# First rows transposed within the attention, first layer between the last routing steps, third set's gathers moved up

## The chip, the cores and the metric

The kernel runs on one core of one Trainium2 chip. The metric is the device time in microseconds (us) of one execution; lower is better. A time is the median of several executions. The engines are PE (TensorE), DVE (VectorE), ACT (ScalarE), POOL (GpSimd) and SP (SyncE, which only issues DMAs here).

## What is computed

A recurrent linear attention over 4 batches, 8 heads, 768 steps and head size 48, and on its output (3072 rows of 384) a mixture of 8 experts with one expert for each row:

```python
for t in range(S):
    cur = np.einsum('bhd,bhe->bhde', u[None] * kt, vt)
    y[:, :, t] = np.einsum('bhd,bhde->bhe', rt, state + cur)
    state = w[None, :, :, None] * state + np.einsum('bhd,bhe->bhde', kt, vt)
...
logits = x @ w_gate
expert_idx = np.argmax(logits, axis=1)
gate_w = probs[np.arange(N), expert_idx]
...
h = np.maximum(np.einsum('ecd,edf->ecf', disp, w1), 0.0)
y = np.einsum('ecf,efd->ecd', h, w2)
out[i] = gate_w[i] * y[expert_idx[i], pos[i]]
```

w1 is 8 x 384 x 1024 and w2 is 8 x 1024 x 384, all in float32.

## The kernel before

**Attention.** The 3072 rows are 24 tiles of 128 steps. The loop `for i in range(NI)` (L617) runs the attention of tile i and, one turn later, the gate of tile i-1. In each turn PE makes the scores of tile i+1 (`scores`, L521), a small product `c` (`mix`, L80 and L82) and, after ACT has copied `c` to `ct` (L87), a second small product, here called the **pull** (L92). DVE copies its result (L93): 8 gate logits of tile i-1, and the factors with which ACT writes the diagonal blocks of tile i+2's score matrix, eight instructions of `diag` (L502). PE then transposes the attention's output of tile i-1 back to rows (`turn`, tile `xp`, L104), and does `values1` (L555) and `values2` (L564) of tile i; ACT copies the outputs (`xs`, L568) and the rows (`xr`, `keep_rows`, L111). DVE masks the next scores (`masks`, L525), scales keys (`prep_keys`, L507; `prep_values`, L513) and keeps the state (`state_of`, L543).

**Routing.** Tiles go through the routing in groups; tiles 22 and 23 are groups by themselves. `route` (L124) is a generator of three parts: DVE finds the maximum and its one-hot `oh` (L127 to L140); PE ranks the rows (`rk`, L145 to L148) from `oh` and the running counts `lane`, which are then advanced (L151); DVE makes the row's slot and the softmax's divisor (L159 to L165). `advance()` runs one part. `scatters` writes the rows to `xsd` in device memory at their slots, by indirect DMA from POOL. `counts` (L178) and `places` (L185) turn the last counts into the row numbers `pidx` which `gather(k)` reads back, by POOL's indirect DMAs, into `xg[k % 2]`.

**Experts.** `PASSES` lists nine sets of rows: set 0 is the first 160 rows of expert 0, gathered already in turn 20 from what tiles 0 to 15 have sent (2 tiles of 128 rows, 80 of each used), set 1 the other 256 of expert 0, sets 2 to 8 are 416 rows each of experts 1 to 7 (4 tiles of 104). For each set `xtrans` transposes the gathered rows in three parts (tile `tp`, L290) and splits each into a high and a low half, `xh` on ACT (L294) and `xl` on DVE (L295); `layer1` makes 8 blocks `a` of 9 matmuls each (L307 to L309, three products for each of 3 parts of the contraction), which ACT and DVE split into `hh` (L312) and `hl` (L313); `layer2` makes three blocks `b` of 24 matmuls (L326 to L328); `finish` transposes them back (`yp`, L342) and scatters the rows to the output (L334). The first layer of set k, block by block, comes before the transposes of set k+1 and the second layer of set k.

**Weights.** `wstream` is a generator: by a plan, one step fetches a slice `wr` from SP (L240, four buffers) and splits earlier ones into high and low halves `ws`, the high on ACT (`CAST`, L248), the low on DVE (L249). For expert 0 one step runs at the end of a turn of the attention; its low half is issued in the next step. The experts after that run one step after each block.

**What sets the order.** The kernel is recorded under a manual schedule: each engine runs its instructions in the order in which the Python code issues them, and waits by semaphores. POOL's indirect DMAs stand in one queue with its arithmetic. PSUM tiles with one tag share buffers: `tp` and the blocks `a` of set 0 take turns in two buffers `a0`, with `u` and `y` as the third.

The end of the attention before: after the last turn come the transposes of set 0 (`acts`), the small product of tile 23 and the first block of layer one, then the pull of tile 23, the ranks of tiles 22 and 23, and the other blocks with `counts`, `places` and `gather(1)` after the second. `gather(k + 1)` stands at the head of the loop over the sets, so `gather(2)` comes after both transposes of set 0's output.

Of the kernel before, what the change touches and what calls it, by code (L numbers as in the profile page):

```python
# [7 lines left out]
F32R = mybir.dt.float32r  # L8
# [5 lines left out]
PSUM = bass.MemoryType.PSUM  # L14
# [20 lines left out]
def rwkv_moe(nc, tc, dmj, rkv, bdc, wv, wu, uv, wg, w1, w2, out, cap):  # L35
# [4 lines left out]
    with ExitStack() as ctx:  # L40
# [175 lines left out]
        with ExitStack() as mc:  # L216
# [7 lines left out]
            psB = pa.enter_context(tc.tile_pool(name="psB", bufs=1, space=PSUM))  # L224
            mc.enter_context(tc.manual_schedule())
            xg = [keep.tile([128, 4, XW], F32, name=f"xg{j}") for j in range(2)]
            wtiles = {}

            def wset(e):
# [387 lines left out]
            for i in range(NI):  # L617
# [37 lines left out]
                    T[i + 2]["bon"] = to  # L655
                xp = turn(i - 1, T[i - 1]["xs"], ps1)
                advance()
                each(prep_values, i + 2)
                state_of(i)
                values1(i)  # L660
                each(diag, i + 2, (0, 1, 2))
# [7 lines left out]
                    advance()  # L669
                if i == 1:  # L670
                    setup_ok(wc)
                next(ws)
                if i == 18:
                    early_places(sm, ps1)
                if i == 20:
# [2 lines left out]
                if i in (9, 13):  # L678
                    nc.gpsimd.memset(xg[i == 13], 0.0)
                T.pop(i - 1)  # L680
            lc.close()
            pa.close()
            psA = mc.enter_context(tc.tile_pool(name="psA", bufs=2, space=PSUM))
            buf = mc.enter_context(tc.tile_pool(name="act", bufs=1, side="right"))
            xh, xl = (buf.tile([128, 3, WL], F32R, name=n) for n in ("xh", "xl"))
            hh, hl = (buf.tile([128, 8, WL], F32R, name=n) for n in ("hh", "hl"))
            yt = buf.tile([128, 3, WL], F32, name="yt")
            scatters(NI)
            acts = [xtrans(0, j) for j in range(3)]
            take(0)  # L690
            c = mix(None, T[NI - 1]["xs"], ps1)
            acts[0]()
            ct = mixed(c, buf)
            acts[1]()
            acts[2]()
            first = layer1(0, 0)
            to = place_of(NI - 1, sm, rows_of)
            pull(c, ct, to)
            xp = turn(NI - 1, T[NI - 1]["xs"], ps1)
            advance()  # L700
            advance()
            rout(NI - 1, sm, ps1, rows_of, "rows")
            advance()
            keep_rows(NI - 1, xp, rows_of)
            first()
            advance()
            scatters(1)
            second = layer1(0, 1)
            advance()
            scatters(NI)  # L710
            counts(ps1)
            places(1, E, cs[:, 0:E], sm)
            gather(1)
            second()
            next(ws)
            next(ws)
            for f in (2, 3):
                layer1(0, f)()
                next(ws, None)
            ac.close()  # L720

            wsp.append(mc.enter_context(tc.tile_pool(name="wsq", bufs=1)))
# [9 lines left out]
            for d in range(3):  # L732
                layer2(0, d)
                next(ws)
            take(1)
            for d in range(3):
                xtrans(1, d)()
            finish(0, 0)
            finish(0, 1)
            for k in range(1, len(PASSES)):  # L740
                if k + 1 < len(PASSES):
                    gather(k + 1)
                for f in range(8):
                    layer1(k, f)()
                    next(ws, None)
                    if k > 1 and 1 <= f <= PASSES[k - 1][4]:
                        finish(k - 1, f - 1)
                if k + 1 == len(PASSES):
                    nc.gpsimd.drain()
                if k + 1 < len(PASSES):  # L750
                    take(k + 1)
                    for d in range(3):
                        xtrans(k + 1, d)()
                        layer2(k, d)
                        next(ws, None)
                        next(ws, None)
                    e = PASSES[k + 1][0] + 1
                    if e < E:
                        ws = wstream(e, PLAN)
                        next(ws)  # L760
                else:
                    layer2_last(k)
# [227 lines left out]
```

## Time and profile before

| what | us |
|---|---|
| median of 3 runs | 401.98 (399.9 to 402.25) |
| profiled execution, its own time | 398.83 |
| its span, from the first to the last instruction | 397.0 |

The profiled execution is one execution of the program; 1.83 us lie outside its span. All times inside it are counted from the span's start. The attention fills the span up to about 130 us, the experts the rest. "Granted clock" is the share of TensorE's 2.4 GHz that it was given: 1.00 is 2.4 GHz, 0.50 is 1.2 GHz. Busy time of a matmul overlaps that of its neighbours, so the step from one start to the next is the better measure of its cost. A wait is put down to the event that came last before the instruction.

### The profile page before, as it was taken

The numbers are of one execution on the slowest core, as the hardware profiler recorded it, in microseconds if no ns is written. First come the engines' busy times: TensorE is split into PE (matmuls) and PEld (weight loads), VectorE is DVE, ScalarE is ACT, GpSimd is POOL, SyncE is SP. The second block draws the span as 40 slices with busy tenths as digits, with TensorE's granted clock in tenths as the row PEclk, the third lists the DMA queues.
The fourth block names the chain that finished last, engine by engine and source line by source line (L and its number), as shares of the span: only waits on it lengthen the run. The fifth ranks groups of instructions, "written<-read, shape, count | busy, mean of one in ns | idle before, by whom it ended". The sixth has DMA issues, their size and how long they took to land.

```text
span 397.0 us, 9469 instructions
## 1 busy us (share of the span) xinstructions
PE 373.5 (94%) x3587; PEld 339.1 (85%) x3590; DVE 238.7 (60%) x574; ACT 203.9 (51%) x556; POOL 136.2 (34%) x199
## 2 busy tenths in 40 slices
PE   7999999999998799689999999999999999999993
PEld 3678777777886699689999999999999999999992
DVE  6897889898986775614745645645645645643210
ACT  3768787778776463414624724724724724722301
POOL 6122639565675321711501601601601601201203
PEclk9999999999999989969999999999999999999998
DMA  8999988888723463830633643644644644500102
GB/s 174 263 244 245 230 228 242 255 233 251 216 88 94 158 192 92 248 78 5 214 108 110 188 140 114 186 143 110 195 138 116 191 140 120 155 4 16 43 1 70
DMA packets 20632, 59.93 MB, mean 151 GB/s; under 512 B 4302, under 2 KB 4450, under 8 KB 20576
## 3 DMA queue, kind: packets, MB, share of 16 engines
q1 hardware_dynamic: 14848, 44.12, 40.6%
q0 software_dynamic: 5600, 14.72, 11.6%
q8 instruction: 30, 0.49, 0.6%
q10 hardware_dynamic: 128, 0.39, 0.4%
q14 instruction: 26, 0.21, 0.2%
HBM read 49.98 MB, written 10.03 MB: 151 GB/s over the span
## 4 chain that ended last, share of the span: by engine, by line
PE 61%; issue 13%; ACT 11%; DVE 7%; DMA 3%; POOL 2%; POOLq 1%; SPq 0%; DVEq 0%; ACTq 0%
PE a L307 8%; PE a L308 8%; PE a L309 8%; PE b L326 7%; PE b L327 7%; PE b L328 7%; ACT s L502 7%; PE a L521 3%; PE y L564 2%; DVE s L525 2%; PE tp L290 2%; PE yp L342 2%; POOL out L334 2%; PE c L92 2%; DMA xg<-xsd,pidx 2%
## 5 line engine op out<-in xcount | busy, mean ns | idle before, releaser
L334 POOL DMA_INDIRECT out<-yo,ids x32 | 32.2, 1008 | 176.2 <-ACT yo L333 174.9
L307 PE MATMUL a<-xh,ws 128*128 128x416 f32 (+1 forms) x216 | 75.7, 350 | 1.0 <-DVE xl L295 1.0
L326 PE MATMUL b<-hh,ws 128*128 128x416 f32 (+2 forms) x216 | 74.5, 345 | 0.0
L312 ACT ACTIVATE hh<-a 128x416 fp32r<-128x416 f32 (+1 forms) x72 | 35.2, 489 | 73.9 <-PE a L309 73.8
L308 PE MATMUL a<-xl,ws 128*128 128x416 f32 (+1 forms) x216 | 73.1, 338 | 0.0
L309 PE MATMUL a<-xh,ws 128*128 128x416 f32 (+1 forms) x216 | 73.1, 338 | 0.0
L328 PE MATMUL b<-hh,ws 128*128 128x416 f32 (+2 forms) x216 | 72.5, 336 | 0.0
L327 PE MATMUL b<-hl,ws 128*128 128x416 f32 (+2 forms) x216 | 72.5, 336 | 0.0
L313 DVE SCALAR_TENSOR_TENSOR hl<-a,hh 128x416 fp32r<-128x416 f32 (+1 forms) x72 | 39.9, 554 | 47.8 <-ACT hh L312 47.1
L249 DVE TENSOR_TENSOR ws<-wr,ws 128x384 fp32r<-128x384 f32 (+1 forms) x112 | 66.8, 612 | 0.2 <-ACT ws L248 0.2
L502 ACT ACTIVATE s<-eye,l 128x128 f32<-128x128 f32 x168 | 53.8, 391 | 20.1 <-DVE l L93 20.1
L248 ACT CAST ws<-wr 128x384 fp32r<-128x384 f32 (+1 forms) x112 | 59.9, 557 | 0.0
L329 DVE COPY yt<-b 128x416 f32<-128x416 f32 (+2 forms) x27 | 14.6, 542 | 70.3 <-PE b L328 70.3
L491 POOL TENSOR_TENSOR P<-dm 112x512 f32<-112x512 f32 x21 | 27.1, 1289 | 48.9 <-DVE dm L507 17.7
L294 ACT CAST xh<-tp 128x416 fp32r<-128x416 f32 (+1 forms) x27 | 12.7, 484 | 60.0 <-PE tp L290 60.0
L307 PEld LDWEIGHTS a<-xh,ws 128*128 128x128 f32 x216 | 41.3, 191 | 1.5 <-DVE xl L295 1.3
L326 PEld LDWEIGHTS b<-hh,ws 128*128 128x128 f32 x216 | 42.0, 194 | 0.2
L327 PEld LDWEIGHTS b<-hl,ws 128*128 128x128 f32 x216 | 41.9, 194 | 0.2
L328 PEld LDWEIGHTS b<-hh,ws 128*128 128x128 f32 x216 | 41.6, 193 | 0.4
L308 PEld LDWEIGHTS a<-xl,ws 128*128 128x128 f32 x216 | 41.4, 192 | 0.5 <-DVE xl L295 0.2
L309 PEld LDWEIGHTS a<-xh,ws 128*128 128x128 f32 x216 | 41.3, 191 | 0.4
L273 POOL DMA_INDIRECT xg<-xsd,pidx x32 | 34.9, 1091 | 13.9 <-issue 6.7
(147 smaller groups left out, 560.4 us busy)
## 6 DMA issues: line engine op xcount, KB each, us to landing
wr<-w SPq DMA_DIRECT2D x24, 512.0 KB, 4.4
wr<-w SPq DMA_DIRECT2D x32, 384.0 KB, 3.4
bd<-bdc SPq DMA_DIRECT2D x24, 384.0 KB, 5.0
dm<-dmj SPq DMA_DIRECT2D x40, 192.0 KB, 4.2
dm<-dmj SPq DMA_DIRECT2D x6, 256.0 KB, 7.7
xg<-xsd,pidx POOLq DMA_INDIRECT x32, 4.6
out<-yo,ids POOLq DMA_INDIRECT x32, 3.7
dm<-dmj ACTq DMA_DIRECT2D x2, 192.0 KB, 4.1
```

The source lines that it names most:

```text
L248: nc.scalar.copy(out=hi, in_=r)
L249: low.append(lambda: nc.vector.tensor_tensor(out=lo, in0=r, in1=hi.bitcast(F32), op=ALU.subtract))
L307: nc.tensor.matmul(a, lhsT=wh, rhs=xh[:, d, :n], start=d == 0, stop=False)
L308: nc.tensor.matmul(a, lhsT=wh, rhs=xl[:, d, :n], start=False, stop=False)
L309: nc.tensor.matmul(a, lhsT=wl, rhs=xh[:, d, :n], start=False, stop=d == 2)
L312: nc.scalar.activation(hh[:, f, :n], a, AF.Relu)
L313: nc.vector.scalar_tensor_tensor(out=hl[:, f, :n], in0=a, scalar=0.0, in1=hh[:, f, :n].bitcast(F32), op0=ALU.max, op1=ALU.subtract)
L326: nc.tensor.matmul(o, lhsT=wh, rhs=hh[:, f, :n], start=f == 0, stop=False)
L327: nc.tensor.matmul(o, lhsT=wh, rhs=hl[:, f, :n], start=False, stop=False)
L328: nc.tensor.matmul(o, lhsT=wl, rhs=hh[:, f, :n], start=False, stop=f == 7)
L334: r = nc.gpsimd.indirect_dma_start(out=out[:, :], out_offset=bass.IndirectOffsetOnAxis(ap=ids[k][0][:qo, i:i + 1], axis=0), in_=yo, in_off ...
L502: nc.scalar.mul(out=s[:, h, p], in_=eye, mul=bon)
```

## The change

Three things are moved; the arithmetic stays as it is.

1. In the attention the weight step `next(ws)` runs after the pull and the transposes of the rows, ahead of `diag`, where it stood at the end of the turn.
2. In the last turn the first two parts of set 0 are transposed and split ahead of `values1`, the third directly after the loop. `xh` and `xl` move to a pool that lives from the start, and the score buffers of PSUM are given to the experts in the middle of that turn. After it come block 0 of layer one, the small product of tile 23, block 1, the pull, the rank of tile 22, block 2, the rank of tile 23, and block 3 after `gather(1)`.
3. `gather(2)` is issued after the first block of set 0's second layer, ahead of set 0's output.

```diff
+            xh, xl = (keep.tile([128, 3, WL], F32R, name=n) for n in ("xh", "xl"))
...
                 advance()
+                next(ws)
                 each(prep_values, i + 2)
+                if i == NI - 1:
+                    pa.close()
+                    psA = mc.enter_context(tc.tile_pool(name="psA", bufs=2, space=PSUM))
+                    acts = [xtrans(0, j) for j in range(2)]
+                    take(0)
+                    acts[0]()
+                    acts[1]()
                 state_of(i)
...
-                next(ws)
...
+            xtrans(0, 2)()
             lc.close()
-            pa.close()
-            psA = mc.enter_context(tc.tile_pool(name="psA", bufs=2, space=PSUM))
             buf = mc.enter_context(tc.tile_pool(name="act", bufs=1, side="right"))
-            xh, xl = (buf.tile([128, 3, WL], F32R, name=n) for n in ("xh", "xl"))
...
+            first = layer1(0, 0)
+            c = mix(None, T[NI - 1]["xs"], ps1)
+            ct = mixed(c, buf)
             scatters(NI)
-            acts = [xtrans(0, j) for j in range(3)]
-            take(0)
-            c = mix(None, T[NI - 1]["xs"], ps1)
-            acts[0]()
-            ct = mixed(c, buf)
-            acts[1]()
-            acts[2]()
-            first = layer1(0, 0)
+            first()
+            second = layer1(0, 1)
             to = place_of(NI - 1, sm, rows_of)
             pull(c, ct, to)
             xp = turn(NI - 1, T[NI - 1]["xs"], ps1)
             advance()
-            advance()
             rout(NI - 1, sm, ps1, rows_of, "rows")
             advance()
             keep_rows(NI - 1, xp, rows_of)
-            first()
+            second()
+            third = layer1(0, 2)
             advance()
-            scatters(1)
-            second = layer1(0, 1)
+            next(ws)
+            advance()
+            third()
             advance()
             scatters(NI)
             counts(ps1)
             places(1, E, cs[:, 0:E], sm)
             gather(1)
-            second()
             next(ws)
-            next(ws)
-            for f in (2, 3):
-                layer1(0, f)()
-                next(ws, None)
+            layer1(0, 3)()
+            next(ws, None)
...
             for d in range(3):
                 layer2(0, d)
                 next(ws)
+                if d == 0:
+                    gather(2)
...
-                if k + 1 < len(PASSES):
+                if 1 < k < len(PASSES) - 1:
                     gather(k + 1)
```

In the orders below a number after a name is the buffer's; line numbers from L227 on are one or a few higher in the changed kernel.

ACT in turn 21 of the attention, before: the row copy, two casts of weights, the copy `ct`, then the next output copies.

```order
L111 COPY xr_121<-xp_2250 128x384
L248 CAST ws_0_1013<-wr_0_1370 128x384
L248 CAST ws_0_1013<-wr_0_1565 128x384
L87 COPY ct<-c 128x128
L568 COPY xs_2368<-y_0_2350 128x2x128
L568 COPY xs_2368<-y_1_2351 128x2x128
```

The same place now:

```order
L111 COPY xr_123<-xp_2252 128x384
L87 COPY ct<-c 128x128
L249 CAST ws_0_979<-wr_0_1522 128x384
L249 CAST ws_0_979<-wr_0_1700 128x384
L569 COPY xs_2374<-y_0_2356 128x2x128
L569 COPY xs_2374<-y_1_2357 128x2x128
```

The casts stand behind `ct` instead of ahead of it; in turns that still have a `diag`, they stand between `ct` and its first six instructions.

PE at the end of the attention, before, from the rank of tiles 20 and 21 on (blocks of layer one are shown by their first matmul):

```order
L148 MATMUL rk_2403<-lane,ones 128x16
...
L564 MATMUL y_1_2410<-s_120,bd_1924 48x128 x2
L290 MATMUL tp_0_2472<-idn,xg_101 128x128 x2
L290 MATMUL tp_1_2475<-idn,xg_101 128x128 x2
L290 MATMUL tp_2_2478<-idn,xg_101 128x128 x2
L82 MATMUL c<-xs_2427,wgz 32x128 x4
L307 MATMUL a_0_2498<-xh,ws_0_1011 128x256
...
L92 MATMUL c<-pick,ct 128x16
...
L145 MATMUL rk_2517<-oh_2446,tri 128x8
...
L145 MATMUL rk_2544<-oh_2535,tri 128x8
...
L307 MATMUL a_1_2551<-xh,ws_0_1011 128x256
```

PE there now:

```order
L148 MATMUL rk_2405<-lane,ones 128x16
L291 MATMUL tp_0_2418<-idn,xg_101 128x128 x2
L291 MATMUL tp_1_2421<-idn,xg_101 128x128 x2
...
L291 MATMUL tp_2_2473<-idn,xg_101 128x128 x2
L308 MATMUL a_0_2485<-xh,ws_0_977 128x256
...
L82 MATMUL c<-xs_2450,wgz 32x128 x4
L308 MATMUL a_1_2510<-xh,ws_0_977 128x256
...
L92 MATMUL c<-pick,ct 128x16
...
L145 MATMUL rk_2529<-oh_2469,tri 128x8
...
L308 MATMUL a_2_2545<-xh,ws_0_977 128x256
...
L145 MATMUL rk_2568<-oh_2561,tri 128x8
```

Block 1 (a_1) now stands ahead of the pull of tile 23, and block 2 (a_2) between the ranks of tile 22 and tile 23, which stood side by side.

DVE over the same stretch, before:

```order
L295 TENSOR_TENSOR xl<-tp_0_2472,xh 128x256
L295 TENSOR_TENSOR xl<-tp_1_2475,xh 128x256
L295 TENSOR_TENSOR xl<-tp_2_2478,xh 128x256
L93 COPY l_2508<-c 128x16
L159 TENSOR_TENSOR ps_2521<-rk_2517,oh_2446 128x8
...
L138 TENSOR_TENSOR oh_2535<-key_2531,km_2533 128x8
L140 TENSOR_TENSOR z_2537<-l_2508,mx_2529 128x8
L313 SCALAR_TENSOR_TENSOR hl<-a_0_2498,hh 128x256
L151 TENSOR_TENSOR lane<-lane,oh_2535 128x8
```

DVE now:

```order
L296 TENSOR_TENSOR xl<-tp_1_2421,xh 128x256
L159 TENSOR_TENSOR ps_2455<-rk_2405,oh_2385 128x16
...
L140 TENSOR_TENSOR z_2471<-l_2396,mx_2463 128x8
L296 TENSOR_TENSOR xl<-tp_2_2473,xh 128x256
L314 SCALAR_TENSOR_TENSOR hl<-a_0_2485,hh 128x256
L93 COPY l_2520<-c 128x16
...
L314 SCALAR_TENSOR_TENSOR hl<-a_1_2510,hh 128x256
...
L138 TENSOR_TENSOR oh_2561<-key_2557,km_2559 128x8
...
L250 TENSOR_TENSOR ws_0_980<-wr_0_1700,ws_0_979 128x384
L151 TENSOR_TENSOR lane<-lane,oh_2561 128x8
```

The third `xl` stands behind two parts of the routing, the low half of block 1 inside the chain of tile 23, and a weight subtraction ahead of the last `lane`.

POOL before, from the last scatters to the gathers of sets 2 (xg_101) and 3 (xg_102):

```order
L172 DMA xsd<-xr_123,slot 24576x400
L273 DMA xg_102<-xsd,pidx 128x400 x2
L334 DMA out<-yo_0_2818,ids_2481 3072x384
L334 DMA out<-yo_1_2827,ids_2481 3072x384
L273 DMA xg_101<-xsd,pidx 104x400 x4
L273 DMA xg_102<-xsd,pidx 104x400 x4
```

POOL there now:

```order
L172 DMA xsd<-xr_125,slot 24576x400
L274 DMA xg_102<-xsd,pidx 128x400 x2
L274 DMA xg_101<-xsd,pidx 104x400 x4
L335 DMA out<-yo_0_2830,ids_2424 3072x384
L335 DMA out<-yo_1_2839,ids_2424 3072x384
L274 DMA xg_102<-xsd,pidx 104x400 x4
```

Set 2's four gathers stand directly behind set 1's two, ahead of the two output scatters for which POOL has to wait.

## Rows read from the trace of the kernel before

**Rows 1.** Page, part 1: busy time, share of the span and instructions of each engine.

```profile
PE 373.5 (94%) x3587; PEld 339.1 (85%) x3590; DVE 238.7 (60%) x574; ACT 203.9 (51%) x556; POOL 136.2 (34%) x199
```

**Rows 2.** Waits of PE, 128 to 397 us: for whom, us in total, times, longest.

```profile
PE tp L290 <- DMA xg<-xsd,pidx: 4.7, 3, 2.4
PE rk L145 <- DVE oh L138: 1.9, 1, 1.9
PE a L307 <- DVE xl L295: 1.0, 1, 1.0
```

**Rows 3.** Timeline of PE, 160 to 180 us: start, us, instruction [idle before <- who ended it].

```profile
164.68 0.25 PE L290 MATMUL tp<-idn,xg 104*128 104x104 f32 x1
...
170.34 0.43 PE L290 MATMUL tp<-idn,xg 104*128 104x104 f32 x1 [0.94 <-DMA xg<-xsd,pidx]
170.47 0.56 PE L326 MATMUL b<-hh,ws 128*128 128x256 f32 x1
...
175.57 0.52 PE L290 MATMUL tp<-idn,xg 104*128 104x104 f32 x4
175.87 0.36 PE L326 MATMUL b<-hh,ws 128*128 128x256 f32 x1
...
178.81 0.52 PE L290 MATMUL tp<-idn,xg 104*128 104x104 f32 x4
```

**Rows 4.** Windows of 2 us; columns PE, PEld, DVE, ACT, POOL busy, PEclk, DMA share, GB/s.

```profile
138.00:140.00 2.00, 2.00 (x13) 2.00 (x13) 1.69 (x7) 1.19 (x3) 0.98 (x1) 0.50 0.31 111
146.00:148.00 2.00, 2.00 (x19) 2.00 (x18) 1.93 (x7) 1.83 (x5) 0.00 (x0) 1.00 0.60 166
168.00:170.00 2.00, 0.43 (x1) 0.18 (x1) 0.00 (x0) 0.00 (x0) 1.70 (x2) 0.63 1.02 283
```

**Rows 5.** Timeline of POOL, 95 to 200 us, around the indirect transfers.

```profile
142.32 1.05 POOL L273 DMA_INDIRECT xg<-xsd,pidx  x1 [2.52 <-DVE ws L249]
...
156.64 0.96 POOL L334 DMA_INDIRECT out<-yo,ids  x1 [11.95 <-ACT yo L333]
...
159.16 1.10 POOL L273 DMA_INDIRECT xg<-xsd,pidx  x1 [0.31 <-issue]
...
163.57 1.08 POOL L273 DMA_INDIRECT xg<-xsd,pidx  x1 [0.30 <-issue]
```

**Rows 6.** Instructions that write or read xg, 110 to 200 us: issue to landing.

```profile
DMA to landing us min/median/max: 2.9/4.6/7.6
```

**Rows 7.** Waits of PE, 25 to 128 us.

```profile
PE c L92 <- ACT ct L87: 3.2, 6, 1.0
```

**Rows 8.** Timeline of ACT, 48 to 72 us and 110 to 150 us.

```profile
55.74 1.86 ACT L502 ACTIVATE s<-eye,l 128x128 f32<-128x128 f32 x6 [0.70 <-DVE l L93]
...
126.92 0.94 ACT L248 CAST ws<-wr 128x384 fp32r<-128x384 f32 x2
127.75 0.29 ACT L87 COPY ct<-c 128x128 f32<-128x128 f32 x1
```

**Rows 9.** Timeline of PE, 112 to 148 us, at the boundary.

```profile
123.65 0.40 PE L92 MATMUL c<-pick,ct 128*128 128x16 f32 x2 [0.68 <-ACT ct L87]
...
128.09 0.40 PE L92 MATMUL c<-pick,ct 128*128 128x16 f32 x2 [0.95 <-ACT ct L87]
...
132.83 0.39 PE L307 MATMUL a<-xh,ws 128*128 128x256 f32 x1 [1.04 <-DVE xl L295]
...
136.73 0.17 PE L145 MATMUL rk<-oh,tri 128*128 128x8 bf16 x1 [1.92 <-DVE oh L138]
...
141.73 0.28 PE L307 MATMUL a<-xh,ws 128*128 128x256 f32 x1
```

**Rows 10.** Timeline of DVE, 128 to 138 us: parts of the routing chain.

```profile
129.07 0.17 DVE L159 TENSOR_TENSOR ps<-rk,oh 128x16 f32<-128x16 f32 x1 [0.37 <-PE rk L148]
...
130.04 0.14 DVE L127 TENSOR_REDUCE mx<-l 128x1 f32<-128x8 f32 x1
...
130.90 1.03 DVE L249 TENSOR_TENSOR ws<-wr,ws 128x384 fp32r<-128x384 f32 x2
```

## The prediction

> **What bounds the kernel now.** I read the page's busy times first, then PE's waits by stage, then the timeline around each wait. PE is busy for 94% of the span [rows 1], and in the experts' part, from 128 us to the end, it waits for other engines in three places only: 4.7 us for the gathers into `xg`, 1.9 us for the one-hot of tile 23, 1.0 us for the third `xl` of set 0 [rows 2]. So the second half is a chain of matmuls: what PE gains before or in it comes off the end, unless another wait takes its place. In the attention PE waits 3.2 us in all for ACT's copy `ct` [rows 7].
>
> The largest hole is at 164.68. There PE begins the four transposes of set 2 and reaches the first matmul of the next `b` block only at 170.47 [rows 3]. The reader is to see why on POOL: set 2's gathers are issued from 159.16 on, behind two output scatters, the first of which waited 11.95 us for `yo`, although POOL was done with set 1's gathers some 12 us earlier [rows 5]. They are issued just when weights of the next expert flow: at 168 to 170 the DMA engines are full, at 283 GB/s, and the granted clock has begun to fall [rows 4]. A gather took up to 7.6 us from issue to landing, 4.6 in the median [rows 6].
>
> **The change part by part.**
>
> *Gathers of set 2.* POOL's order puts them directly behind set 1's. Set 1's first gather began at 142.32 [rows 5]; its second and the four of set 2 follow at steps of about 1.47 us (from 159.16 to 163.57 in three steps, [rows 5]), so the last is issued at about 149.7 and landed at the latest, with the longest landing of rows 6, at 157.3. PE asks for them at 164.68, or about 3 us sooner if the boundary gains what I expect. The slack is 4 us or more, and I take the wait as gone. What it gives: from 164.68 to 170.47 are 5.79 us, where four transposes between two `b` blocks normally take 0.30 (175.57 to 175.87): 5.49 us. Behind the hole the clock is low: the 24 matmuls of that block took 5.10 us (170.47 to 175.57), those of the next one 2.94 (175.87 to 178.81) [rows 3]: 2.16 us more. Together 7.65. Lower bound 5.5, if the clock falls there for another reason. Next late behind this wait is nothing that the rows show; `gather(3)` keeps its place and lands within set 1's first layer or soon after it.
>
> The Trainium skill ("DMA: Bandwidth & Descriptors", section "Issuing engines are not separate DMA queues") says that DMAs of all issuing engines end up on the same 16 DMA engines and interleave. That speaks against the change, since the new place is not empty either; the trace agrees in kind, for the gathers were slowest in the fullest windows. By it the early gathers could slow weights; the second rival gives that a price.
>
> In the new place, about 143 to 151, the DMA share is 0.60 at 166 GB/s in the window of 146 to 148 [rows 4]. Set 2 is 416 rows of 1600 bytes, 0.67 MB; at the 283 GB/s of the full window that is 2.4 us of all engines. It can shift weights by so much; ACT and DVE have no wait for weights there, so I put it at nothing, and at 2.4 us as the upper bound.
>
> *Weight steps in the attention.* A cast ahead of `ct` delays the pull. For tiles 21 and 22 two casts took 0.94 us, and `ct` followed directly (126.92, 127.75, [rows 8]); PE waited 0.68 and 0.95 us for it [rows 9]. Behind `ct` the casts cost nothing there: no `diag` follows in these turns. The first wait goes whole, 0.68. Of the second I take 0.6, since PE's product `c` has to end first too (bounds 0 and 0.95). Of the other waits of rows 7, 3.2 - 0.68 = 2.5 us (the 0.95 lies outside that window), DVE's masks and weight subtractions are close behind in most of these turns, so I take 0.5, bounds 0 and 2.5. Where `diag` follows, the cast lands in a gap: ACT idled 0.70 us there, waiting for DVE's copy [rows 8], against some 0.5 to 0.6 for one cast (half of 0.94, [rows 8]). Cover gone, nine casts would cost up to 0.5 each; that is a rival. The low halves on DVE keep their number and move within the turn; the state behind them is needed a turn later. Sum: 0.5 + 0.68 + 0.6 = 1.8, bounds 0.7 and 4.1.
>
> *Boundary.* From the pull of tile 22 (128.09) to block 3's end, which is the start of block 4 (141.73), PE takes 13.64 us [rows 9]. Of that 1.04 and 1.92 are waits [rows 9], and about 3 us ran at half the granted clock (138 to 140 at 0.50, [rows 4]), which by 2.94 to 5.10 is a loss of 1.3. The work itself is 13.64 - 2.96 - 1.3 = 9.4, the same in both kernels. Waits in the new order:
> - the third `xl` stands on DVE behind two parts of the routing, 129.07 to 130.90, 1.83 us [rows 10]; PE has `values1`, `values2`, a transpose and six matmuls in the meantime. Bounds 0 and 1.83, taken 0.5.
> - the one-hot of tile 23: PE waited 1.92 with nothing between the two ranks. Now block 2, nine matmuls of 2.94 / 24 = 0.12, fills 1.1 of it, but DVE has the low half of block 1 inside the chain. Taken 1.1, bounds 0.8 and 1.9.
> - `counts` waits for the last `lane`, which now stands behind one weight subtraction, half of 1.03 [rows 10]: 0.5. Blocks queued behind `counts` on PE wait with it.
>
> That is 2.1 us against 2.96. If the clock stays at 2.4 GHz, the boundary takes 9.4 + 2.1 = 11.5 and gains 2.1; if it falls to 1.2 GHz for 3 us again, 0.8. Before, it fell after a wait of 1.92 us, with another of 1.04 some 3 us earlier [rows 9]; now the gaps are shorter but close together. I take 1.5, bounds -0.5 and 2.5.
>
> The Trainium skill ("TensorE: Matmul & The Clock Gate", section "Why this matters for your kernels") holds that the clock falls after gaps longer than any that the trace has at this boundary. The trace disagrees: there the longest was 1.92 us. By the page the clock would stay up and the sum would be 0.6 us better.
>
> *Sum.* 7.65 + 1.8 + 1.5 = 10.95 us. From the profiled execution's 398.83 that makes 387.9. The median of the runs shown is 401.98, 3.15 above the profiled one, and I take off the same: 391.0. The own range: gains from 5.5 + 0.7 - 0.5 = 5.7 to 7.65 + 4.1 + 2.5 = 14.2, so 387.7 to 396.3; the three runs spread over 2.35 us, of which I add a little at both ends.
>
> **The rivals.** A measurement of this kernel tells about 1%, 4 us, from no change.
>
> First: *the boundary gives nothing*, because DVE's serial chain for tile 23 sets its end, however the blocks are laid around it, and the clock falls as before. For it: `xl`, two low halves and a weight subtraction now stand in or ahead of that chain. Against: three blocks are done before its end, not one. Then 7.65 + 1.8 = 9.45 with the boundary at zero, 392.5; with -0.5, 393.0.
>
> Second: *the hole moves*. The early gathers share the DMA engines with the next expert's weights, a cast on ACT waits for its slice, the transposes' high halves wait behind it, and PE idles and loses its clock as before; or the gathers land late in any case. It decides when a gather of set 2 takes over 11 us from issue, or a weight slice comes 3 us late. Rows 6 show 7.6 at most, rows 4 a DMA share of 0.60. All of the 7.65 gone leaves 3.3: 398.7.
>
> Third: *casts ahead of `diag`* become what the masks wait for, 9 x 0.5 = 4.5 us lost. For it: the gap of 0.70 is hardly longer than a cast. Gain 10.95 - 4.5 - 0.5 = 6.0: 396.0.
>
> Fourth, *slower*: the granted clock falls at the boundary and stays at 1.2 GHz through the first expert's matmuls. At 5.10 against 2.94 us a block, 42% of such time is lost; it decides from 10.95 / 0.42 = 26 us at the low level, that is, from the boundary through set 0 and most of set 1. With 40 us it costs 17: 408. Against it: both low stretches ended under dense matmuls after some 3 and 5 to 7 us.
>
> That the change doesn't do what it says is excluded by the orders, but for the landing, which is the second rival.
>
> **How the numbers follow.** Forecast 0.62; boundary without gain 0.23; hole moves 0.07; casts 0.06; slower 0.02. The forecast and the first and third rivals are all faster by over 1% (0.91, and a little of the second rival: 0.92); the second at 398.7 is mostly within 1%: 0.06; slower 0.02. The range goes from 387.0 to 396.5 and leaves out the second and fourth rivals and the edges of the others.
>
> **What would show it.** In the changed profile: no PE wait for `xg`, and the granted clock at 1.00 where set 2 is transposed; set 2's gathers issued within some 8 us of set 1's and landed well ahead of their transposes. No PE wait for `ct` at tiles 21 and 22 beyond 0.4. From the pull of tile 22 to block 4 about 11.5 us, or 12.8 with a low clock. PE waits at the third `xl` and at the ranks of about 0.5 and 1.1. It would be wrong if PE waits at transposes or `hh` in the experts' part, if the masks wait longer for `diag`, or if the set 1 transposes begin to wait for their own gathers.

## The result, and the profile after

The changed kernel took 396.75 us in the median of 4 runs (395.92 to 397.02), the kernel before 402.12 us (4 runs, 399.9 to 402.87): a ratio of 0.9872 with an interval of 0.983 to 0.9914. That is a gain of 5.4 us where 10.95 was forecast, and 0.25 us above the top of the range. Its profiled execution took 397.02 us with a span of 395.3.

The waits of PE from 128 us to the end, us in total, times, longest; they answer to [rows 2]:

```profile
PE a L308 <- issue: 2.0, 1, 2.0
PE c L92 <- ACT ct L87: 1.7, 1, 1.7
PE rk L145 <- DVE oh L138: 1.1, 1, 1.1
PE ct L180 <- ACT hh L313: 0.4, 1, 0.4
```

The 4.7 us for `xg` are gone, the ranks wait 1.1 instead of 1.9, and the third `xl` is not among the waits. But two new waits stand there that no order of instructions explains at first sight: 1.7 us for a `ct` and 2.0 us for nothing that the profile shows.

PE's timeline around set 2, as in [rows 3]:

```profile
167.93 0.39 PE L308 MATMUL a<-xh,ws 128*128 128x256 f32 x1 [2.04 <-issue]
...
170.61 0.52 PE L291 MATMUL tp<-idn,xg 104*128 104x104 f32 x4
170.91 0.36 PE L327 MATMUL b<-hh,ws 128*128 128x256 f32 x1
...
173.83 0.52 PE L291 MATMUL tp<-idn,xg 104*128 104x104 f32 x4
```

The four transposes take 0.30 us and the block behind them 2.92, with the clock at 2.4 GHz (granted 1.00 from 168 to 172). The gathers did exactly what the prediction's first term says. POOL's timeline shows where they went, as in [rows 5]:

```profile
148.65 1.05 POOL L274 DMA_INDIRECT xg<-xsd,pidx  x1 [2.47 <-DMA xsd<-xr,slot]
150.00 1.26 POOL L274 DMA_INDIRECT xg<-xsd,pidx  x1 [0.30 <-issue]
151.56 1.08 POOL L274 DMA_INDIRECT xg<-xsd,pidx  x1 [0.30 <-issue]
...
155.80 1.06 POOL L274 DMA_INDIRECT xg<-xsd,pidx  x1 [0.31 <-issue]
159.83 0.98 POOL L335 DMA_INDIRECT out<-yo,ids  x1 [2.97 <-ACT yo L334]
```

Set 2's four gathers, 151.56 to 155.80, are issued 14.8 us and more before PE asks for them at 170.61. But PE arrives there at 170.61, and at 164.68 before [rows 3]. Most of what the closed hole gave, 5.93 of 7.67 us, was lost ahead of it.

To see where, I cut every profiled execution at the same five places of PE's timeline: the pull of tile 22, the first `b` block, set 1's transposes, set 2's transposes, and the transposes one block later. Cut so, before against after (us):

| stretch | before | after | gained |
| --- | --- | --- | --- |
| start to pull of tile 22 | 128.09 | 131.26 | -3.17 |
| pull to first `b` block | 17.90 | 17.24 | 0.66 |
| to set 1's transposes | 8.56 | 9.24 | -0.68 |
| to set 2's transposes | 10.13 | 12.87 | -2.74 |
| to the end of the block behind them | 10.89 | 3.22 | 7.67 |
| to the end of the span | 221.43 | 221.47 | -0.04 |
| span | 397.0 | 395.3 | 1.7 |

The forecast's 7.65 stands in the fifth row as 7.67. What took it back are mainly 3.17 us in the attention and 2.74 in set 1's first layer, where the change was to gain or to do nothing.

### The profile page after: what moved, and what is told of

It reads as the page before. It is cut to its first block, busy times and chain, and to the rows that moved or that the text cites. A ratio compares the mean times of both kernels' runs of the same rounds, so it can differ in the third digit from the quotient of the medians.

```text
span 395.3 us, 9463 instructions
## 1 busy us (share of the span) xinstructions
PE 375.1 (95%) x3587; PEld 338.4 (86%) x3590; DVE 237.2 (60%) x574; ACT 204.4 (52%) x556; POOL 137.7 (35%) x199
## 3 DMA queue, kind: packets, MB, share of 16 engines
q0 software_dynamic: 5600, 14.72, 11.5%
## 4 chain that ended last, share of the span: by engine, by line
PE 74%; issue 12%; ACT 5%; DVE 3%; POOL 2%; DMA 1%; POOLq 1%; another core or an unknown queue 0%; SPq 0%; ACTq 0%; DVEq 0%
PE a L310 8%; PE a L309 8%; PE a L308 8%; PE b L327 7%; PE b L328 7%; PE b L329 7%; PE y L565 6%; PE a L522 6%; PE y L556 3%; PE xp L104 3%; PE c L92 2%; ACT s L503 2%; PE c L82 2%; PE tp L291 2%; PE u L534 2%
## 5 line engine op out<-in xcount | busy, mean ns | idle before, releaser
L327 PE MATMUL b<-hh,ws 128*128 128x416 f32 (+2 forms) x216 | 73.4, 340 | 0.0
L328 PE MATMUL b<-hl,ws 128*128 128x416 f32 (+2 forms) x216 | 71.7, 332 | 0.3 <-issue 0.3
L329 PE MATMUL b<-hh,ws 128*128 128x416 f32 (+2 forms) x216 | 71.5, 331 | 0.0
L250 DVE TENSOR_TENSOR ws<-wr,ws 128x384 fp32r<-128x384 f32 (+1 forms) x112 | 67.6, 618 | 2.3 <-ACT ws L249 2.3
L308 PEld LDWEIGHTS a<-xh,ws 128*128 128x128 f32 x216 | 40.7, 188 | 3.3 <-issue 2.4
L328 PEld LDWEIGHTS b<-hl,ws 128*128 128x128 f32 x216 | 40.8, 189 | 0.8 <-issue 0.5
L329 PEld LDWEIGHTS b<-hh,ws 128*128 128x128 f32 x216 | 40.6, 188 | 0.4
L327 PEld LDWEIGHTS b<-hh,ws 128*128 128x128 f32 x216 | 40.8, 189 | 0.2
L310 PEld LDWEIGHTS a<-xh,ws 128*128 128x128 f32 x216 | 40.6, 188 | 0.4
```

What stands on the lines that cost most here:

```text
L250: low.append(lambda: nc.vector.tensor_tensor(out=lo, in0=r, in1=hi.bitcast(F32), op=ALU.subtract))
L308: nc.tensor.matmul(a, lhsT=wh, rhs=xh[:, d, :n], start=d == 0, stop=False)
L310: nc.tensor.matmul(a, lhsT=wl, rhs=xh[:, d, :n], start=False, stop=d == 2)
L327: nc.tensor.matmul(o, lhsT=wh, rhs=hh[:, f, :n], start=f == 0, stop=False)
L328: nc.tensor.matmul(o, lhsT=wh, rhs=hl[:, f, :n], start=False, stop=False)
L329: nc.tensor.matmul(o, lhsT=wl, rhs=hh[:, f, :n], start=False, stop=f == 7)
```

## Experiments

Two theories. **Parts**: the three edits take from each other, the boundary above all. **Stops**: the parts add up, but the two profiled executions differ in something that is not of the kernel's order. In the after trace two turns between 104 and 117 us last 6.0 to 6.2 us instead of 4.7 to 4.8; ACT's copies there show it:

```profile
108.69 0.65 ACT L569 COPY xs<-y 128x256 f32<-128x256 f32 x2 [1.28 <-PE a L522]
...
114.72 0.68 ACT L569 COPY xs<-y 128x256 f32<-128x256 f32 x2 [1.27 <-PE a L522]
```

**Each part alone**, on one chip, where the kernel before took 397.73 us (15 runs); a trace of it was taken beside them.

> The kernel before once more, for a second trace. If the stops that the changed kernel's trace shows in the attention (ACT's output copies 1.3 us late twice, the copy ct 1.5 us late) come with the change, they are absent here and the pull of tile 22 starts near 128.1 us again. If they come and go between executions, this trace has one or two like them, and its time lies near 402 rather than 398.8.

> Only the gathers of set 2 are moved. Theory A (the prediction's term): the hole of 5.5 us and its low clock of 2.2 us go, 7.65 us faster, about 394.4. Theory B (the hole moves: transfers collide elsewhere): ACT or PE stops near the next full stretch of the DMA engines, and only 3 to 5 us are left, about 397 to 399.

```diff
             for d in range(3):
                 layer2(0, d)
                 next(ws)
+                if d == 0:
+                    gather(2)
...
-                if k + 1 < len(PASSES):
+                if 1 < k < len(PASSES) - 1:
                     gather(k + 1)
```

> Only the weight steps in the attention are moved. Prediction's term: 1.8 us faster, about 400.3, with waits for ct gone at tiles 21 and 22. Rival: the casts ahead of diag hold up the masks, 0 to 4 us slower, 402 to 406.

```diff
                 xp = turn(i - 1, T[i - 1]["xs"], ps1)
                 advance()
+                next(ws)
                 each(prep_values, i + 2)
...
-                next(ws)
                 if i == 18:
```

> Only the end of the attention is rearranged. Prediction's term: 0.8 to 2.1 us faster, about 400.5. Rival (the boundary gives nothing, since the routing of tile 23 starts later): 0 to 2 us slower, 402 to 404; scatter of tile 23 and set 1's gathers later than 138.8 and 142.3.

The third is the whole change without these two edits. Measured: gathers 390.86 us, ratio 0.9817 (0.9782 to 0.9852), a gain of 6.9; weight steps 395.09, 0.9921 (0.9894 to 0.9948), a gain of 2.6; boundary 398.39, 1.0012 (0.9992 to 1.0032), nothing. The forecast had 7.65, 1.8 and 1.5. No trace of this chip has the two long turns, and the kernel before is 4 us faster here than in the first measurement. In the kernel with the gathers alone, PE's timeline at set 2 reads

```profile
164.00 0.52 PE L290 MATMUL tp<-idn,xg 104*128 104x104 f32 x4
164.30 0.36 PE L326 MATMUL b<-hh,ws 128*128 128x256 f32 x1
...
167.22 0.52 PE L290 MATMUL tp<-idn,xg 104*128 104x104 f32 x4
```

so the hole is closed, and PE comes to it no later than before (164.68 in [rows 3]). The Trainium skill ("DMA: Bandwidth & Descriptors", section "Issuing engines are not separate DMA queues") spoke against the new place, since the DMAs of all issuing engines share the DMA engines; on this chip the stretch in which they now run, from the first `b` block to set 1's transposes, takes 8.56 us with and without them. On the chips that follow below, the four traces with the early gathers and the boundary as before have 8.78 to 8.91 us there, the two of the kernel before 8.56 and 8.57, so up to 0.35 us may be their price.

Why the boundary gives nothing is in two places. PE's timeline in the kernel with the boundary alone:

```profile
128.18 0.40 PE L92 MATMUL c<-pick,ct 128*128 128x16 f32 x2 [0.95 <-ACT ct L87]
...
132.95 0.39 PE L308 MATMUL a<-xh,ws 128*128 128x256 f32 x1 [0.66 <-ACT xh L295]
...
133.75 0.39 PE L309 MATMUL a<-xl,ws 128*128 128x256 f32 x1 [0.41 <-DVE xl L296]
...
135.72 0.29 PE L92 MATMUL c<-pick,ct 128*128 128x16 f32 x2
...
138.78 0.17 PE L145 MATMUL rk<-oh,tri 128*128 128x8 bf16 x1 [1.09 <-DVE oh L138]
139.40 0.18 PE L180 MATMUL ct<-lane,ones 128*128 128x8 bf16 x1 [0.43 <-ACT hh L313]
...
140.63 0.28 PE L308 MATMUL a<-xh,ws 128*128 128x256 f32 x1
```

and in the kernel before, traced on the same chip:

```profile
127.42 0.39 PE L92 MATMUL c<-pick,ct 128*128 128x16 f32 x2 [0.95 <-ACT ct L87]
...
132.16 0.39 PE L307 MATMUL a<-xh,ws 128*128 128x256 f32 x1 [1.04 <-DVE xl L295]
...
133.34 0.29 PE L92 MATMUL c<-pick,ct 128*128 128x16 f32 x2
...
136.06 0.17 PE L145 MATMUL rk<-oh,tri 128*128 128x8 bf16 x1 [1.92 <-DVE oh L138]
...
139.57 0.27 PE L307 MATMUL a<-xh,ws 128*128 128x256 f32 x1
```

The last line of each is the first matmul of block 4. The one-hot waits 1.09 and the third `xl` 0.41, as forecast (1.1 and 0.5), but block 0 now waits 0.66 for `xh` as well, which I had not counted, and tile 23 is pulled 7.54 us behind tile 22 instead of 5.92: its chain stands behind a block and those two waits. And its last scatter comes later (issued at 141.51, at 138.17 in the kernel before), which ACT meets one stage on:

```profile
144.50 0.62 ACT L249 CAST ws<-wr 128x512 fp32r<-128x512 f32 x1 [2.22 <-DMA xsd<-xr,slot]
```

That cast writes the next expert's first weights, and its engine waits 2.22 us for the last scatter to land. The source suggests the reason, argued and not tried: the tile lies where the attention's rows lay. DVE's low halves queue behind it, and PE pays at the first `b` block:

```profile
148.11 0.39 PE L328 MATMUL b<-hl,ws 128*128 128x256 f32 x1 [0.32 <-DVE hl L314]
```

From the first `b` block to set 1's transposes that kernel takes 9.25 us, 0.69 more than the kernel before on that chip (8.56).

**The parts in pairs**, on another chip, where the kernel before took 402.44 us (19 runs, 397.3 to 405.07).

> The changed kernel once more, beside its parts. Parts so far against before: gathers 0.982, weight steps 0.992, boundary 1.001; if they add, about 0.975, some 388 us where before takes 397.7. If the stops in the attention that its first trace showed (pull of tile 22 at 131.3 us) belong to the change, they stand at the same places again and the ratio is near 0.987. If they were that execution's or that chip's, the pull starts near 125.5 and the ratio is near 0.975.

> Gathers and weight steps without the boundary. If the two add: 0.974, about 387.5 us, the fastest of all. If they get in each other's way: 0.982 or more, no better than the gathers alone.

> Gathers and boundary without the weight steps. If they add: 0.983, about 391. If the boundary is what costs (set 1's gathers, the last scatter and a cast on ACT that waits for it come later, and then meet the early gathers): 0.988 to 0.992, and ACT waits about 2 us for a scatter.

> Weight steps and boundary without the gathers. If they add: 0.993, about 395. If they get in each other's way: 1.000 or more, and the attention's trace has the stops of the changed kernel.

Their edits are those above, put together; the last is the change without the move of the gathers. Measured: the whole change 0.9893 (0.9791 to 0.9995), gathers and steps 0.9851 (0.9741 to 0.9961), gathers and boundary 0.9896 (0.9857 to 0.9934), steps and boundary 0.9911 (0.9868 to 0.9955). The intervals overlap, so the times alone don't tell the pairs from each other. The traces tell more: all four have the two long turns, and pull tile 22 at 130.9 to 131.9 us. The kernel with gathers and steps has the steps-only kernel's instructions up to there, which pulled at 125.30. The same instructions came 5.6 us later on this chip.

**Both kernels on that chip, traced.** The kernel `pull_first` is the change with tile 23's product ahead of block 0 and its pull ahead of block 1:

```diff
-            first = layer1(0, 0)
             c = mix(None, T[NI - 1]["xs"], ps1)
             ct = mixed(c, buf)
             scatters(NI)
+            first = layer1(0, 0)
             first()
-            second = layer1(0, 1)
             to = place_of(NI - 1, sm, rows_of)
             pull(c, ct, to)
+            second = layer1(0, 1)
```

> The kernel before, traced once more beside the changed one on the same chip. If the stops seen at 104 to 117 us in the changed kernel's traces belong to the execution or the chip, this trace has them too on a chip whose median for the kernel before is near 402, and the pull of tile 22 then comes at about 130 instead of 128; on a chip near 397.7 neither kernel has them. If they come from the changed kernel's order of instructions, the kernel before has none here while the changed kernel again has two turns of about 6 us in that stretch.

> The changed kernel. If the boundary part is worth nothing and the other two add up, it stands where the kernel with the gathers and the weight steps alone stands, within 0.002, at a ratio near 0.974 on a chip near 397.7 (6.9 + 2.6 = 9.5 us gained) or near 0.986 on a chip near 402. If the boundary part costs something only beside the others, it stands 0.003 or more above that kernel. By the prediction it stands 0.004 below it.

> The gathers of set 2 moved and the weight steps moved, the boundary as before. The two parts alone gained 6.9 and 2.6 us; if they add up, 0.974 to 0.977. If they take from each other (the same execution stops, or a later hole that both uncover), no better than the gathers alone, 0.982.

> The changed kernel with tile 23's gate product ahead of block 0 and its pull ahead of block 1, so that block 0 covers the copy ct and block 1 the one-hot. If the boundary's gain is eaten because the blocks push the chain of tile 23 back (pull of tile 23 at 7 to 8 us behind that of tile 22 in the changed kernel, 5.9 before), that distance shrinks by about 1 to 1.5 us, the last scatter and the gathers of set 1 come as much earlier, and the time falls by 0.5 to 1.5 us (a ratio 0.001 to 0.004 below the changed kernel). If PE's own work between pull and block 4 sets the end, whatever the order, the distance shrinks and the time stays within 0.001 of the changed kernel's.

Measured against 401.47 us for the kernel before (10 runs): the change 0.982 (0.978 to 0.986), gathers and steps 0.9836 (0.9796 to 0.9877), pull first 0.9842 (0.9805 to 0.9879). The trace of the kernel before settles whose the long turns are. ACT's timeline in it:

```profile
108.22 0.65 ACT L568 COPY xs<-y 128x256 f32<-128x256 f32 x2 [1.24 <-PE a L521]
```

and DVE's at the same moment:

```profile
108.26 0.16 DVE L191 TENSOR_TENSOR pen<-pos,ct 128x4 f32<-128x4 f32 x1 [1.27 <-PE a L521]
108.46 0.16 DVE L192 SCALAR_TENSOR_TENSOR pidx<-pen,pos 128x4 int32<-128x4 f32 x1
```

The kernel before has them too, here with tile 22 pulled at 131.94; in its trace of the first chip the same two instructions start at 106.32 and 106.33 with no idle time before them. Two engines that wait for two products of PE start within 0.04 us, after 1.24 and 1.27 us of idle time. I call these the stops. The changed kernel has no part in them.

**A third and a fourth chip.**

> The kernel before, to tell which kind of chip this is. On a chip of the first kind its median is near 397.7, tile 22 is pulled at 127 to 128 us and no two turns of about 6 us stand at 104 to 117 us; on one of the second kind the median is 401 to 402, the pull comes at about 132 and the two long turns are there.

> The changed kernel. If the missing gain is the stops of the chips of the second kind, then on a chip of the first kind gathers (6.9) and weight steps (2.6) add up with a boundary worth nothing: 9.5 us, about 388.2 from 397.7, a ratio near 0.976, the pull of tile 22 at 125 to 126 us and no PE wait above 1.2 us from 150 to 172. If the parts take from each other whatever the chip, the ratio stays at 0.982 to 0.989. On a chip of the second kind: 0.982 to 0.987 again, with the pull at 131 to 132, and the question stays where it is.

> The changed kernel with the boundary as before. On a chip of the first kind 0.976 as well if the boundary part is worth nothing beside the other two, and 0.003 to 0.005 above the changed kernel if the boundary gives the 1 to 2 us that the stretch from the pull of tile 22 to the first b block shows in the traces. On a chip of the second kind 0.984 within 0.003.

> Tile 23's gate product and pull ahead of blocks 0 and 1. Last time it stood 0.002 above the changed kernel with overlapping intervals, though tile 23 was pulled 5.2 us behind tile 22 and not 6.8. If the chain of tile 23 sets the end of the boundary on a chip without stops, it is 0.5 to 1.5 us faster than the changed kernel; if PE's own work sets it, equal within 1 us.

> The changed kernel once more. On a chip whose kernel before stands near 397.7: 388 to 389 and a ratio near 0.976 if the stops took the missing gain; 0.982 or more if the parts take from each other. On a chip whose kernel before stands at 401 to 403: 0.982 to 0.987.

> Set 2's gathers moved, nothing else. On the first kind of chip 6.9 us again, 0.982 to 0.983. On the second kind the hole in the kernel before is shorter: from set 2's first transpose to the end of the block behind it 7.48 and 5.81 us in two traces, against 3.22 where the gathers are early, so 2.6 to 4.3 us and 0.989 to 0.994, if the gathers are worth what the hole costs; 0.982 there too if they are worth the same on every chip.

Both chips have the stops. On the one (before 402.86, 11 runs): the change 0.9867 (0.9828 to 0.9907), gathers and steps 0.9861 (0.9808 to 0.9913), pull first 0.9818 (0.9774 to 0.9862). On the other (before 401.54, 15 runs): the change 0.9857 (0.981 to 0.9903), the gathers alone 0.9906 (0.9874 to 0.9937). This last is the result that tells most: the same edit gave 6.9 us where there are no stops and 3.8 us here, and the two intervals do not overlap. PE's timeline shows why. In the kernel before, on the third chip, the hole is

```profile
171.46 0.25 PE L290 MATMUL tp<-idn,xg 104*128 104x104 f32 x1
172.24 0.31 PE L290 MATMUL tp<-idn,xg 104*128 104x104 f32 x1 [0.53 <-DMA xg<-xsd,pidx]
172.83 0.31 PE L290 MATMUL tp<-idn,xg 104*128 104x104 f32 x1 [0.28 <-DMA xg<-xsd,pidx]
173.42 0.31 PE L290 MATMUL tp<-idn,xg 104*128 104x104 f32 x1 [0.27 <-DMA xg<-xsd,pidx]
```

1.96 us from the first transpose to the last, against 5.66 in [rows 3], and the clock stays up behind it. The windows from 172 us, columns as in [rows 4]:

```profile
172.00:174.00 2.00, 1.20 (x7) 0.86 (x8) 0.96 (x2) 0.56 (x3) 1.68 (x2) 1.00 0.90 303
174.00:176.00 2.00, 2.00 (x19) 2.00 (x18) 0.96 (x2) 0.63 (x2) 1.70 (x2) 1.00 0.71 186
```

Two things make it shorter. PE comes to set 2 later: set 1's stretch takes 11.46 us where it takes 10.13 without stops. And the gathers are there sooner after their issue, as POOL's timeline of the same trace shows at the first of them:

```profile
164.59 1.10 POOL L273 DMA_INDIRECT xg<-xsd,pidx  x1 [0.31 <-issue]
```

From this issue PE takes 6.87 us to the first transpose (171.46) and 8.83 to the last (173.42); in [rows 5] and [rows 3] it is 5.52 and 11.18 (159.16 to 164.68 and to 170.34). So of the 3.70 us by which the hole is shorter, 1.35 are PE's later arrival and 2.35 the sooner landing; why the gathers land sooner there stays open.

All executions side by side, cut as above; "low" says that a window of 2 us between 132 and 148 had a granted clock under 0.9:

| kernel | pull of tile 22 | to `b` | to set 1 | to set 2 | block behind | span |
| --- | --- | --- | --- | --- | --- | --- |
| no stops: before | 128.09 | 17.90 low | 8.56 | 10.13 | 10.89 | 397.0 |
| before again | 127.42 | 16.41 | 8.56 | 10.13 | 10.35 | 394.9 |
| gathers | 127.38 | 17.93 low | 8.56 | 10.13 | 3.22 | 389.0 |
| steps | 125.30 | 17.51 low | 8.57 | 10.12 | 10.76 | 393.8 |
| boundary | 128.18 | 16.72 | 9.25 | 10.12 | 9.52 | 395.4 |
| stops: before, third | 131.94 | 19.39 low | 8.57 | 10.66 | 7.48 | 399.7 |
| before, fourth | 131.93 | 19.51 low | 8.56 | 11.46 | 5.81 | 398.6 |
| gathers, fifth | 133.43 | 19.58 low | 8.88 | 10.61 | 3.24 | 397.4 |
| gathers and steps | 130.89 | 19.81 low | 8.78 | 10.58 | 3.22 | 395.1 |
| the same, third | 131.76 | 17.53 low | 8.91 | 10.61 | 3.23 | 393.6 |
| the same, fourth | 132.94 | 16.00 | 8.78 | 12.85 | 3.21 | 395.4 |
| steps and boundary | 131.60 | 17.47 low | 9.25 | 11.35 | 4.50 | 395.8 |
| gathers and boundary | 131.93 | 18.24 low | 8.62 | 10.61 | 3.23 | 394.6 |
| after | 131.26 | 17.24 low | 9.24 | 12.87 | 3.22 | 395.3 |
| after again | 131.34 | 17.49 low | 8.60 | 10.63 | 3.23 | 393.1 |
| after, third | 131.54 | 15.94 | 9.22 | 12.19 | 3.21 | 393.8 |
| after, fourth | 132.72 | 15.97 | 9.27 | 13.19 | 3.23 | 396.2 |
| after, fifth | 130.51 | 17.48 low | 8.56 | 10.63 | 3.23 | 391.9 |
| pull first | 130.61 | 16.99 low | 8.57 | 12.05 | 3.23 | 392.7 |
| pull first, again | 130.77 | 15.48 | 9.19 | 11.42 | 3.23 | 391.8 |

The kernel `pull_first` pulls tile 23 at 5.17 us behind tile 22 (6.77 in the change on the same chip), as meant, but the rank of tile 23 still waits 1.09 us for its one-hot in both its traces, and its time cannot be told from the change's: 0.002 above it on one chip, 0.005 below it on the other, with overlapping intervals. No version beat the change on the chips with stops by more than its interval. On the chip without them only single parts were run.

## Why the prediction was wrong

**The step that failed** is the last of the sum: "The median of the runs shown is 401.98, 3.15 above the profiled one, and I take off the same". It takes the other executions for the profiled one plus a constant. As far as the runs show, they are another kind of execution. The profiled one had no stops; the two of the kernel before that were traced with stops took 401.41 and 400.28 us, and those without 398.83 and 396.62. The timed runs of 399.9 to 402.87 lie with the former, which is inferred, since no trace of them was taken; the changed kernel's profiled execution, which is one of its four timed runs, has the stops. In such executions the terms have other sizes. One reading ahead of the sum was short, without changing it: in [rows 2] PE waits in a fourth place after 128 us, 0.9 us at the pull of tile 22, which the weight steps' term counts.

**Gathers of set 2, 7.65.** The mis-sized term of the sum: right in mechanism and in size for the execution that it was read from (7.67 in the trace, 6.9 us timed alone on the chip without stops), mis-sized for the timed ones: 3.8 us. The fifth column shows the same: from 10.89 and 10.35 to 3.22 without stops, 7.67 and 7.13; from 7.48 and 5.81 with them, 4.26 and 2.59. The low clock, 2.16 of the term, is not there at all in one of these two.

**Weight steps, 1.8.** Right: 2.6 us alone without stops. With stops it is the difference between the ratios of two kernels that were not run on one chip: 0.9849, the mean of three for gathers and steps, against 0.9906 for the gathers, 2.3 us of 402, and uncertain by as much. The waits for `ct` in the attention fell from 4.3 us in the kernel before, traced on the same chip, to 1.9; the row for the steps alone, 25 to 128 us, as in [rows 7]:

```profile
PE c L92 <- ACT ct L87: 1.9, 4, 0.5
```

The third rival, casts ahead of `diag`, didn't come: between 25 and 128 us DVE's masks waited 8.2 us in all for ACT's `diag` in that kernel and in the kernel before on the same chip.

**Boundary, 1.5.** Mis-sized: 1.0012 alone, and beside the other two parts the change stood 0.4 us above the kernel without it in all three comparisons (395.93 and 395.52, 394.72 and 394.37, 397.62 and 397.25), which is within the intervals, so nothing. The first rival's number was right here. Its reason, that DVE's chain for tile 23 sets the end, is not shown: with tile 23 pulled 1.6 us sooner behind tile 22 (`pull_first`) the time did not move by more than the intervals. The waits named in the forecast came in size, but the pull of tile 23 came later, block 0 waited for `xh`, and a wait that I had not looked for, ACT's cast behind the last scatter's landing, gave back up to 0.7 us at the `b` blocks. From the pull of tile 22 to block 4 it took 12.45 us at full clock (128.18 to 140.63 with the boundary alone), not 11.5: the waits were 2.59 us (0.66, 0.41, 1.09 and 0.43) instead of 2.1, and the rest 9.86 instead of 9.4. The kernel before takes 12.15 (127.42 to 139.57) in an execution in which the clock stays up, 2.96 of waits and 9.19 of the rest, so "the same in both kernels" was wrong for the rest. With stops the stretch to the first `b` block is 2.6 us shorter in the mean of five against two, but there the kernel before has two low stretches and the change at most one, and 0.4 to 0.8 us come back in each of the two stretches behind it.

**Added up** with these sizes, 3.8 + 2.3 - 0.4 = 5.7 us, a ratio of 0.986, which is the mean of the five ratios of the change (0.9872, 0.9893, 0.982, 0.9867, 0.9857). That is no test of adding, because 2.3 and 0.4 are themselves differences between such kernels. The three parts run alone, 3.8 with stops and 2.6 and -0.7 without, give 5.7 as well. On the chip of the pairs, half the sum of the three pairs' gains is 6.9 us, and the change itself gained 4.3 and 7.2 there (0.9893 and 0.982). So the runs are in line with adding, but their intervals are 1.5 to 4.5 us wide to either side. One row speaks against it: with steps and boundary in place the block behind set 2 took only 4.50 us, so the gathers could gain no more than 1.3 there. The theory that the parts take from each other is not needed, but not excluded. By these sizes, of the 10.95, 3.85 went because the hole is shorter with stops, and 1.9 because the boundary gives nothing; 0.5 came back from the steps. Without stops the three parts alone sum to 6.9 + 2.6 - 0.7 = 8.8 us, 389 from 397.7. This was not run: the changed kernel met no such chip.

**The clock.** In the prediction a page of the Trainium skill ("TensorE: Matmul & The Clock Gate", section "Why this matters for your kernels") stood against the trace, since it wants longer gaps than the boundary has. The runs go on disagreeing with it: the granted clock fell there in 14 of 20 traces, 0.50 at the lowest, and no wait of PE from 126 to 150 us is longer than 1.92 us in any of them. Only the five traces without stops count for this in full, since in the others PE's records may not show where it stood still; there the clock fell in three. But the trace that I set against the page was no rule either. The kernel before, traced again with the same two waits (1.04 and 1.92), kept the clock; its window, as in the first of [rows 4]:

```profile
138.00:140.00 2.00, 2.00 (x19) 2.00 (x18) 2.00 (x6) 1.27 (x4) 0.97 (x1) 1.00 0.24 75
```

So the low clock, 1.3 us in the boundary's term, comes in some executions of this kernel and not in others, and taking it from one trace was a matter of luck.

## What to carry to other kernels

A term read from one trace holds for executions like that one. Where the profiled time lies below all timed runs, as 398.83 below 399.9 to 402.25, don't shift the sum by the difference: take a second trace first, and ask of each hole whether it would be shorter if PE came to it later, or if the transfers it waits for landed sooner. Work that is put ahead of a serial chain pays for its cover with the chain's later end, and part of that can be paid stages later: here a cast waited 2.22 us for the chain's last scatter, because, as argued from the source and not tried, its tile lies in the chain's memory.

## What the runs showed of the hardware

Chips differ: the kernel before took 397.73 us on one and 401.5 to 402.9 on three others, and the traces differ by stops. On the three, PE's consumers stand idle for a product that PE's records have already ended: twice at 104 to 117 us, for 1.2 to 1.3 us, in all 14 traces taken on these three chips, whichever the kernel, and in the first trace of the changed one, and in none of the other five; and again in set 1, there for 0.7 to 2.8 us. The 2.0 us without a cause in the changed kernel's profile, at 167.93, stand behind such a stop: ACT's `hh` there had come at 167.03 after 2.76 us of idle time. ACT's timeline of the change on the third chip shows three in a row:

```profile
164.70 0.38 ACT L313 ACTIVATE hh<-a 128x256 fp32r<-128x256 f32 x1 [1.48 <-PE a L310]
...
166.87 0.38 ACT L313 ACTIVATE hh<-a 128x256 fp32r<-128x256 f32 x1 [1.38 <-PE a L310]
...
169.09 0.39 ACT L313 ACTIVATE hh<-a 128x256 fp32r<-128x256 f32 x1 [1.44 <-PE a L310]
```

The granted clock reads 1.00 throughout, and PE's own records show no stop as long at the same place (1.16 us at most here, 0.50 and 0.68 at 104 to 117 us in the kernel before on the second chip). That the delay is PE's, and not its consumers', is suggested by ACT and DVE starting together, and the semaphore events of the traces show it: in that trace of the kernel before, PE signalled the four products that its records end at 106.39, 106.60, 106.72 and 107.81 only at 108.15 to 108.40; in its first trace the same four were signalled within 0.04 us of their ends (106.49 to 107.91). What holds PE's products up stays open. In three of five traces of the change with stops, set 1's stretch is 12.2 to 13.2 us against 10.6 to 11.5 in the two of the kernel before; whether the change brings more stops there, or the few traces only fell so, is not settled (gathers and steps had 12.85 once as well).
